# Attention and two mixtures of experts on one core: the first batch of attention by itself with host-laid operands, and a last dense expert without GpSimd splits

## The chip, the core and the metric

The kernel runs on one NeuronCore of a Trainium2 chip. The metric is the device time of one execution in microseconds (us). Before the change the median of three runs is 691.0 us.

The engines are named as in the profile: PE (TensorE, matrix products), PEld (its weight loads), DVE (VectorE), ACT (ScalarE), POOL (GpSimd) and SP (SyncE, which here only issues transfers). Each engine takes its instructions in the order of the program and waits, at the head of its queue, for what that instruction needs.

## The reference

Three stages follow each other. Sizes: 2 batches, 8 heads, 576 positions, head size 64; 1152 tokens of 512 features; 4 dense and 8 routed experts of 1024 hidden features.

```python
# attention, per batch and head (D = 64, scale = 1/8)
q_d, k_d, v_d = means over groups of 4 positions
out_up = np.repeat(softmax(scale * q_d @ k_d.T) @ v_d, 4, axis=positions)
mask = np.abs(pos[:, None] - pos[None, :]) < 4
out = out_up + softmax(np.where(mask, scale * q @ k.T, -1e9)) @ v
# dense experts, x of (1152, 512)
out = sum over e of p[:, e:e + 1] * (np.maximum(x @ w1[e], 0) @ w2[e])    # p: domain_probs, normalized
# routed experts
logits = (x / |x|) @ (emb / |emb|).T / tau
e = argmax(logits); out = softmax(logits)[e] * (np.maximum(x @ w1[e], 0) @ w2[e])
```

## The kernel before

**Precision.** All products are made in fp32. A weight or activation is split into a rounded half `hi` and the rest `lo`, and three products stand for one. `Weights.halves` (L378) makes one half-chunk (128x512) of a split: ACT writes `hi` (L390) and DVE or POOL writes `lo` (L394). Weights come in chunks of 512 KB into four `raw` buffers and are split into a ring of 13 slots; when both halves of a chunk are split, the next load is issued on SP (L374).

**Attention** (class `Attention`, L30). A unit is one batch and two heads; there are 8 units, 4 to a batch. The work of a unit is cut into 39 pieces, and the list `ROUND` is an order written out by hand: round i goes through the list and does each piece `name` for unit i - lag. `run` (L50) is a generator that makes one piece at a time. For a unit, k and q are loaded as rows (L72), turned on TensorE (twelve transposes of 96x128, L107), and copied out as `kT` and `qT` by ACT and DVE (L121, L127; q is scaled there). POOL adds groups of four positions of k, q and v (L142, L143, L157, L159). TensorE makes the banded scores of 9 blocks in two banks (five and four) and the pooled scores (L162, L187); DVE takes maxima, ACT the exponentials with their sums, DVE inverts the sums (L239, L240), POOL scales the weights (L251), TensorE turns them (L264, L281), ACT and DVE copy them out, TensorE multiplies by v (L306, L319), DVE adds (L332), and ACT and DVE split the result into `xh` and `xl` (L345, L350).

**Attention and the dense work.** At first attention runs alone: 257 of the 312 pieces, until all units of the first batch are done and most of the others well on. Then the dense experts begin. Expert 0 has chunks of 2, 2, 3 and 2 token tiles; the first two need the first batch only. They are 32 steps: `first_half` is one `l1` (12 matmuls), `second_half` is the `l2` of the f before. The other 55 pieces of attention are spread over the first 24 of these steps:

```python
while done < min(rest, -(-rest * (step + 1) // 24)):
    next(run)
    done += 1
if W.half < 2 * n_a:
    W.halves(1, "a", "v")
```

`l1` (L497) is evicted by ACT (L510) and DVE (L511), and `l2` (L513) adds over f = 0 to 7 into banks that L526 or L528 writes out.

**The last dense expert and the routing.** Experts 1 to 3 have three chunks of three tiles. In expert 3 the routing of a finished chunk runs beside the next one. `chunk_jobs` (L927) makes 16 lists of jobs, two for each f, and `step_jobs` does one list in each half of an f. A list can hold dot products of the tokens with the expert rows on DVE (`dots`, L743), the norms on POOL (L644 to L649), `choose` (L748), `ranks` on TensorE, `places` on DVE (L789: the one-hot tables `ohp` and `ohc`, L800 to L802), `enter` on TensorE (L809) and `early_tile`, which gathers the rows of the first two routed tiles with POOL (L854). The array `at` says in which list each job stands. In the same f's, ten chunks of weights of the routed experts are split, ACT for `hi` and POOL for `lo`. After the last dense step come the turns of the gathered rows (L1043), the last `l2`, and the routing of the last chunk, where logits are made on TensorE (L717, L732) and two more chunks are split (`W.halves(4, "vvaa", "p")`).

**The routed experts** follow, with layers at L1055 and L1023, tiles of 128 tokens and a branch for small counts.

Of the kernel before, what the change touches and what calls it, by code (L numbers as in the profile page):

```python
# [26 lines left out]
NRAW = 4  # L27


class Attention:  # L30
# [4 lines left out]
    ROUND = [  # L35
        ("value_a", 4), ("value_b", 4), ("value_d", 4), ("pool_v", 3), ("keep_q", 2), ("scores_a", 2), ("exp_b", 3),
        ("pool_k", 2), ("max_d", 3), ("sum_l", 3), ("scores_b", 2), ("lo", 5), ("max_a", 2), ("keep_d", 4),
        ("exp_d", 3), ("load_q", 1), ("pool_q", 2), ("exp_a", 2), ("scale_a", 3), ("scale_b", 3), ("sum_d", 3),
        ("scores_d", 2), ("turn_pa", 3), ("keep_pa", 3), ("load_vw", 2), ("scale_d", 3), ("add_a", 4), ("turn_pb", 3),
        ("add_b", 4), ("hi", 4), ("turn_pd", 3), ("turn_k", 1), ("turn_q", 1), ("load_k", 0), ("load_vg", 1),  # L40
        ("keep_pb", 3), ("keep_k", 1), ("keep_pd", 3), ("max_b", 2),
    ]

    def __init__(self, nc, cst, ld, wk, bank, q, k, v, xh, xl, pT):
        self.nc, self.cst, self.ld, self.wk, self.bank = nc, cst, ld, wk, bank
        self.q, self.k, self.v, self.xh, self.xl, self.pT = q, k, v, xh, xl, pT
        self.units = [(b, hp) for b in range(B) for hp in range(H // 2)]
        self.st = {}

    def run(self):  # L50

        rounds = len(self.units) + max(lag for _, lag in self.ROUND)
        for i in range(rounds):
            for name, lag in self.ROUND:
                u = i - lag
                if 0 <= u < len(self.units):
                    getattr(self, name)(u, self.st.setdefault(u, {}))
                    yield name, u
# [7 lines left out]
    def load_k(self, u, d):  # L66
        d["kn"] = self.load_rows(u, self.k, "kn")

    def load_q(self, u, d):
        d["qn"] = self.load_rows(u, self.q, "qn")  # L70

    def load_rows(self, u, src, tag):  # L72
        b, hp = self.units[u]
        t = self.ld.tile([96, 6, 2, D], F32, tag=tag, name=tag, bufs=2)
        for h in range(2):
            self.nc.sync.dma_start(out=t[:, :, h, :], in_=src[b, 2 * hp + h].rearrange("(j r) d -> j r d", r=6))
        return t

    def load_vg(self, u, d):
        nc, ld = self.nc, self.ld  # L80
        b, hp = self.units[u]
        vg = ld.tile([72, 2, 2, 4 * D], F32, tag="vg", name="vg", bufs=2)
        for h in range(2):
            nc.sync.dma_start(
                out=vg[:, :, h, :], in_=self.v[b, 2 * hp + h].rearrange("(a j r) d -> j a (r d)", a=2, r=4)
            )
        d["vg"] = vg

    def load_vw(self, u, d):
        nc, ld = self.nc, self.ld  # L90
        b, hp = self.units[u]
        vw = ld.tile([72, 9, 2, D], F32, tag="vw", name="vw", bufs=2)
        for h in range(2):
            off = ((b * H + 2 * hp + h) * S + 60) * D
            nc.sync.dma_start(
                out=vw[:, 1:8, h, :],
                in_=bass.AP(tensor=self.v.tensor, offset=off, ap=[[D, 72], [64 * D, 7], [1, D]]),
            )
        vs = self.v[b, 2 * hp:2 * hp + 2]
        nc.sync.dma_start(out=vw[0:68, 0], in_=vs[:, 0:68, :].rearrange("h p d -> p h d"))  # L100
        nc.sync.dma_start(out=vw[0:68, 8], in_=vs[:, 508:576, :].rearrange("h p d -> p h d"))
        d["vw"] = vw

    def turn(self, src, spots):
        ident = self.cst["ident"]
        for r, (t, o) in enumerate(spots):
            self.nc.tensor.transpose(t[:, o:o + 96], src[:, r].rearrange("p h d -> p (h d)"), ident[0:96, 0:96])  # L107

    def turn_k(self, u, d):
        d["tk"] = self.bank(), self.bank()  # L110
        self.turn(d["kn"], [(d["tk"][0], 96 * r) for r in range(5)] + [(d["tk"][1], 0)])

    def turn_q(self, u, d):
        d["tq"] = self.bank()
        self.turn(d["qn"], [(d["tk"][1], 96 + 96 * r) for r in range(4)] + [(d["tq"], 96 * r) for r in range(2)])

    def spread(self, T, t, o, r0, r1):
        src = t[:, o:o + 96 * (r1 - r0)].rearrange("p (r j) -> p r j", j=96)
        return T.rearrange("p (j r) -> p r j", r=6)[:, r0:r1, :], src

    def keep_k(self, u, d):  # L121
        kT = self.wk.tile([128, S], F32, tag="kT", name="kT", bufs=1)
        for t, o, r0, r1, e in ((d["tk"][0], 0, 0, 5, "a"), (d["tk"][1], 0, 5, 6, "a")):
            self.copy(e, *self.spread(kT, t, o, r0, r1))
        d["kT"] = kT

    def keep_q(self, u, d):  # L127
        qT = self.wk.tile([128, S], F32, tag="qT", name="qT", bufs=1)
        for t, o, r0, r1, e in ((d["tk"][1], 96, 0, 4, "a"), (d["tq"], 0, 4, 6, "v")):
            dst, src = self.spread(qT, t, o, r0, r1)  # L130
            if e == "a":
                self.nc.scalar.activation(out=dst, in_=src, func=AF.Copy, scale=0.125)
            else:
                self.nc.vector.tensor_scalar(out=dst, in0=src, scalar1=0.125, scalar2=None, op0=ALU.mult)
        d["qT"] = qT

    def fours(self, engine, T, out):

        e = self.nc.gpsimd if engine == "p" else self.nc.vector
        Tv = T.rearrange("p (g r) -> p g r", r=4)  # L140
        t = self.wk.tile([128, 144, 2], F32, tag="pt", name="pt")
        e.tensor_tensor(t, Tv[:, :, 0:2], Tv[:, :, 2:4], op=ALU.add)  # L142
        e.tensor_tensor(out, t[:, :, 0], t[:, :, 1], op=ALU.add)  # L143

    def pool_k(self, u, d):
        d["kd"] = self.cst["kd"][u % 2]
        self.fours("p", d["kT"], d["kd"][:, 0:144])

    def pool_q(self, u, d):
        d["qd"] = self.cst["qd"][u % 2]  # L150
        self.fours("p", d["qT"], d["qd"][:, 0:144])

    def pool_v(self, u, d):
        vg = d["vg"]
        e = self.nc.gpsimd if "p" == "p" else self.nc.vector
        t = self.wk.tile([72, 2, 2, 128], F32, tag="pv", name="pv")
        e.tensor_tensor(t, vg[:, :, :, 0:128], vg[:, :, :, 128:256], op=ALU.add)  # L157
        vd = self.wk.tile([72, 2, 2, D], F32, tag="vd", name="vd", bufs=2)
        e.tensor_tensor(vd, t[:, :, :, 0:64], t[:, :, :, 64:128], op=ALU.add)  # L159
        d["vd"] = vd  # L160
# [20 lines left out]
    def scores_a(self, u, d):  # L181
        self.scores(d, 0, 5)

    def scores_b(self, u, d):
        self.scores(d, 5, 9)
# [11 lines left out]

    def max_a(self, u, d):
        d["mx"] = self.wk.tile([128, 9], F32, tag="mx", name="mx", bufs=2)
        self.nc.vector.tensor_reduce(out=d["mx"][:, 0:5], in_=d["s0"], axis=AX.X, op=ALU.max, negate=True)  # L200

    def max_b(self, u, d):
        self.nc.vector.tensor_reduce(out=d["mx"][:, 5:9], in_=d["s5"], axis=AX.X, op=ALU.max, negate=True)

    def max_d(self, u, d):
        m = self.wk.tile([128, 3], F32, tag="mxd", name="mxd", bufs=2)
        self.nc.vector.tensor_reduce(out=m, in_=d["sd"], axis=AX.X, op=ALU.max, negate=True)
        self.nc.vector.tensor_scalar(out=m, in0=m, scalar1=1.0 / 16, scalar2=None, op0=ALU.mult)
        d["mxd"] = m

    def exp(self, P, src, bias, sm, scale=1.0):
# [4 lines left out]
    def exp_a(self, u, d):  # L216
        d["P"] = self.wk.tile([128, 9, 72], F32, tag="P", name="P", bufs=2)
        d["sm"] = self.wk.tile([128, 9], F32, tag="sm", name="sm", bufs=2)
        for i in range(5):
            sm = d["sm"][:, i:i + 1] if i < 5 else None  # L220
            self.exp(d["P"][:, i], d["s0"][:, i], d["mx"][:, i:i + 1], sm)

    def exp_b(self, u, d):
        for i in range(5, 9):
            sm = d["sm"][:, i:i + 1] if i < 5 else None
            self.exp(d["P"][:, i], d["s5"][:, i - 5], d["mx"][:, i:i + 1], sm)

    def exp_d(self, u, d):
        d["Pd"] = self.wk.tile([128, 3, 144], F32, tag="Pd", name="Pd", bufs=2)
        d["smd"] = self.wk.tile([128, 3], F32, tag="smd", name="smd", bufs=2)  # L230
        for i in range(3):
            sm = d["smd"][:, i:i + 1] if i < 3 else None
            self.exp(d["Pd"][:, i], d["sd"][:, i], d["mxd"][:, i:i + 1], sm, 1.0 / 16)

    def weights(self, P, sm, known, weight):

        if known < sm.shape[1]:
            self.nc.vector.tensor_reduce(out=sm[:, known:], in_=P[:, known:], axis=AX.X, op=ALU.add)
        self.nc.vector.tensor_scalar(out=sm, in0=sm, scalar1=1e-9, scalar2=weight, op0=ALU.add, op1=ALU.mult)  # L239
        self.nc.vector.reciprocal(sm, sm)  # L240
        return sm

    def sum_l(self, u, d):
        d["rc"] = self.weights(d["P"], d["sm"], 5, 1.0)

    def sum_d(self, u, d):
        d["rcd"] = self.weights(d["Pd"], d["smd"], 3, 4.0)

    def scale(self, engine, P, rc):
        e = self.nc.gpsimd if engine == "p" else self.nc.vector  # L250
# [1040 lines left out]
```

## Time and profile before

| | before |
|---|---|
| median of 3 runs | 691.0 us (689.84 to 691.18) |
| the profiled execution | 684.17 us, span 682.4 us, mean granted clock 0.997 |
| busy, share of the span | PE 95%, PEld 84%, DVE 51%, ACT 38%, POOL 21% |
| transfers | 73.58 MB in 53790 packets, of them 32286 under 512 B |

The span is the time from the first to the last instruction of the profiled execution. A row of the profile names the line, the engine, the operation, output and inputs with their shapes, the count, and then busy time, the mean of one in ns, and the idle time of the engine just before with what ended it. Busy times of matmuls overlap, so the distance between two starts is the better measure of what one costs. Times in rows count from the start of the span.

### The profile page before, as it was taken

To read this page: it belongs to the slowest core of one execution; us is meant where nothing else is said; L and a number is where in the kernel's file an instruction comes from. 1 tells how busy PE (TensorE), PEld (TensorE's weight loads), DVE (VectorE), ACT (ScalarE), POOL (GpSimd) and SP (SyncE) were. 2 spreads that over 40 slices of the span, in tenths; PEclk is the share of its full clock that TensorE was granted. 3 is DMA by queue.
4 is the path that set the end of the run, shared out by engine and by line. 5 is a ranking of instruction groups with operands and counts; after the bars stand their busy time and mean duration, and the time that the engine had idled before them with its cause. 6 is when DMAs were issued, how large, how long until landed. Compare 5 with 4: busy or idle time off the path is not lost. (4 is left out here: it accounts for less than half of the span.)

```text
span 682.4 us, 11487 instructions
## 1 busy us (share of the span) xinstructions
PE 648.9 (95%) x4287; PEld 574.6 (84%) x4287; DVE 346.3 (51%) x825; ACT 260.9 (38%) x653; POOL 145.1 (21%) x203
## 2 busy tenths in 40 slices
PE   5898999999999999999999999999799999999996
PEld 4677888998999999999999999999698877788775
DVE  2887763314442132442132327979663178499851
ACT  3777632112331111231111222243242368488752
POOL 4888411100000000000000001747441122112111
PEclk9999999999999999999999999999899999999999
DMA  8984430001231001130011116151562156499600
GB/s 222 214 190 117 110 97 2 2 0 37 88 123 62 1 12 50 30 130 27 1 31 63 62 63 200 60 177 62 180 250 79 32 187 214 163 324 361 240 20 30
DMA packets 53790, 73.58 MB, mean 108 GB/s; under 512 B 32286, under 2 KB 37678, under 8 KB 53696
## 3 DMA queue, kind: packets, MB, share of 16 engines
q1 hardware_dynamic: 51392, 66.09, 30.4%
q0 software_dynamic: 2304, 6.33, 3.2%
q8 instruction: 48, 0.79, 0.5%
q14 instruction: 46, 0.38, 0.2%
HBM read 66.10 MB, written 7.09 MB: 107 GB/s over the span
## 5 line engine op out<-in xcount | busy, mean ns | idle before, releaser
L520 PE MATMUL psb<-wh,hT 128*128 128x512 f32 x576 | 198.1, 396 | 0.0
L511 DVE SCALAR_TENSOR_TENSOR hT<-psb,hT 128x384 fp32r<-128x384 f32 (+1 forms) x104 | 54.7, 526 | 221.3 <-ACT hT L510 221.1
L510 ACT ACTIVATE hT<-psb 128x384 fp32r<-128x384 f32 (+1 forms) x104 | 48.5, 467 | 290.2 <-PE psb L506 290.1
L506 PE MATMUL psb<-xh,wh 128*128 128x384 f32 (+1 forms) x416 | 135.3, 325 | 0.0
L506 PE MATMUL psb<-xl,wh 128*128 128x384 f32 (+1 forms) x416 | 134.8, 324 | 0.0
L506 PE MATMUL psb<-xh,wl 128*128 128x384 f32 (+1 forms) x416 | 134.7, 324 | 0.0
L520 PEld LDWEIGHTS psb<-wh,hT 128*128 128x128 f32 x576 | 108.9, 189 | 20.9 <-issue 0.4
L520 PE MATMUL psb<-wl,hT 128*128 128x512 f32 x288 | 113.7, 395 | 0.0
L394 POOL TENSOR_TENSOR wl<-raw,wh 128x512 fp32r<-128x512 f32 x24 | 31.8, 1357 | 306.3 <-ACT wh L390 299.7
L506 PEld LDWEIGHTS psb<-xh,wh 128*128 128x128 f32 x416 | 78.1, 188 | 4.3
L506 PEld LDWEIGHTS psb<-xl,wh 128*128 128x128 f32 x416 | 78.2, 188 | 4.1
L506 PEld LDWEIGHTS psb<-xh,wl 128*128 128x128 f32 x416 | 78.2, 188 | 0.0
L394 DVE TENSOR_TENSOR wl<-raw,wh 128x512 fp32r<-128x512 f32 x108 | 72.6, 718 | 4.5 <-ACT wh L390 3.7
L390 ACT CAST wh<-raw 128x512 fp32r<-128x512 f32 x126 | 70.8, 624 | 0.1
L520 PEld LDWEIGHTS psb<-wl,hT 128*128 128x128 f32 x288 | 54.5, 189 | 7.9
L1055 PE MATMUL psb<-wh,gx 128*128 128x256 f32 x288 | 58.2, 288 | 0.3 <-ACT gx L1045 0.2
L1023 PE MATMUL psb<-wh,hT 128*128 128x512 f32 x160 | 53.9, 399 | 0.8 <-issue 0.5
L1055 PEld LDWEIGHTS psb<-wh,gx 128*128 128x128 f32 x288 | 46.2, 189 | 2.1 <-issue 1.3
L1055 PE MATMUL psb<-wl,gx 128*128 128x256 f32 x144 | 35.9, 283 | 0.0
L1023 PEld LDWEIGHTS psb<-wh,hT 128*128 128x128 f32 x160 | 30.1, 188 | 6.6 <-ACT hT L1006 0.5
L1023 PE MATMUL psb<-wl,hT 128*128 128x512 f32 x80 | 31.5, 394 | 0.0
L1055 PEld LDWEIGHTS psb<-wl,gx 128*128 128x128 f32 x144 | 27.2, 189 | 0.4
(250 smaller groups left out, 840.7 us busy)
## 6 DMA issues: line engine op xcount, KB each, us to landing
raw<-in_moe_w_dram SPq DMA_DIRECT2D x66, 512.0 KB
late_raw<-in_moe_w_dram SPq DMA_DIRECT2D x20, 512.0 KB
acc<-in_moe_w_dram SPq DMA_DIRECT2D x10, 512.0 KB
kn<-in_k_dram SPq DMA_DIRECT2D x16, 144.0 KB
qn<-in_q_dram SPq DMA_DIRECT2D x16, 144.0 KB
vg<-in_v_dram SPq DMA_DIRECT2D x16, 144.0 KB
rows<-acc SPq DMA_DIRECT2D x9, 256.0 KB
vw<-in_v_dram SPq DMA_DIRECT2D x16, 126.0 KB
```

The lines of the kernel that those rows point to most:

```text
L390: nc.scalar.copy(hi[:, c], t[:, c])
L394: lo_eng.tensor_tensor(lo[:, c], t[:, c], hi[:, c].bitcast(F32), op=ALU.subtract)
L506: nc.tensor.matmul(t, a[:, kk, fs], b_[:, kk, xs], start=(n == 0), stop=(n == 11))
L510: nc.scalar.activation(out=hi, in_=t, func=AF.Relu)
L511: nc.vector.scalar_tensor_tensor(out=lo, in0=t, scalar=0.0, in1=hi.bitcast(F32), op0=ALU.max, op1=ALU.subtract)
L520: nc.tensor.matmul(ys[t], a[:, ts], b_[:, f % 2, :], start=(f == 0 and j == 0), stop=(f == 7 and j == 2))
L1023: nc.tensor.matmul(y, gh[:, f, a], b_[:, f % 2, :], start=(n == 0), stop=(n == 23))
L1055: nc.tensor.matmul(dst, a[:, kk], w[:, kk, :], start=(n == 0), stop=(n == 11))
```

## The change

The host lays q and k out as [128, 576] for two heads, features on the partitions, and v as the two tables that the kernel reads; q, k and v of a unit come in two loads each, and the turns and copies of q and k go. The scale of q moves into the exponentials. `pool_q` becomes a reduction on DVE; sums and maxima are done by halves; `keep_d` and both parts of `dT` go to ACT. `ALONE` (34 pieces a unit) is the order for the four units of the first batch, which run alone to their end; `BESIDE` (36 pieces) is the order for the four units of the second batch, two pieces ahead of the dense work and the rest spread over 28 of the 32 steps. Four half-chunks are split in the alone part. In expert 3 the splits go from POOL to DVE, 11 chunks at places given by `AHEAD`, one chunk more after the counts; the routing of chunk 1 takes its third tile's logits on TensorE, and its later steps stand two or three lists earlier.

```diff
...
-    ROUND = [
...
+    ALONE = [
+        ("max_a", 1), ("sum_a", 2), ("scale_a", 2), ("value_d", 4), ("keep_d", 4), ("pool_v", 2),
+        ("turn_pa", 3), ("exp_d", 2), ("sum_b", 2), ("turn_pd", 3), ("value_b", 4), ("scores_a", 0), ("sum_d", 2),
+        ("add_a", 4), ("turn_pb", 3), ("add_b", 4), ("keep_pa", 3), ("keep_db", 3), ("pool_q", 0), ("pool_k", 0),
+        ("scores_b", 0), ("exp_a", 1), ("keep_8", 3), ("value_a", 3), ("scale_b", 2), ("keep_da", 3), ("scale_d", 2),
+        ("max_b", 1), ("max_d", 1), ("hi", 4), ("keep_pb", 3), ("scores_d", 0), ("lo", 4), ("exp_b", 1),
     ]
...
+    BESIDE = [
+        ("keep_pb", 6), ("scores_b", 4), ("max_b", 4), ("pool_k", 3), ("scores_a", 3), ("pool_v", 5), ("exp_a", 4),
...
+    def load_qk(self, u, d):
...
+        t = self.ld.tile([128, 2, S], F32, tag="qk", name="qk", bufs=3)
+        self.nc.sync.dma_start(out=t[:, 1, :], in_=self.k[b, hp])
+        self.nc.sync.dma_start(out=t[:, 0, :], in_=self.q[b, hp])
+        d["qT"], d["kT"] = t[:, 0, :], t[:, 1, :]
...
+        self.nc.vector.tensor_reduce(
+            out=d["qd"][:, 0:144], in_=d["qT"].rearrange("p (g r) -> p g r", r=4), axis=AX.X, op=ALU.add
+        )
...
+    def top(self, m, s, scale):
+
+        self.nc.vector.tensor_reduce(out=m, in_=s, axis=AX.X, op=ALU.max)
+        self.nc.vector.tensor_scalar(out=m, in0=m, scalar1=-scale, scalar2=None, op0=ALU.mult)
...
+    def sum_a(self, u, d):
+        self.inverse(d["sm"][:, 0:4], 1.0)
+
+    def sum_b(self, u, d):
+        self.nc.vector.tensor_reduce(out=d["sm"][:, 4:9], in_=d["P"][:, 4:9], axis=AX.X, op=ALU.add)
+        self.inverse(d["sm"][:, 4:9], 1.0)
...
+        self.copy("a", d["dT"][:, a].rearrange("p h (c q) -> p h c q", c=3), tv)
...
-        self.copy("v", d["od"], d["vo"][:, 0:144])
+        self.copy("a", d["od"], d["vo"][:, 0:144])
...
+        half = H // 2
+        W.ahead = 0
+        for name, u in (("load_qk", 0), ("load_qk", 1), ("load_qk", 2), ("load_v", 0), ("load_v", 1)):
+            att.load(name, u)
+        for name, u in att.run(att.ALONE, range(half)):
+            if name == "scores_d" and u == 0:
+                for name, u in (("load_qk", 3), ("load_v", 3), ("load_v", 2)):
+                    att.load(name, u)
                 W.load_to(NRAW)
...
+            elif name == "lo" and u < 3:
+                W.halves((1, 1, 2)[u], "a", "v")
+        W.ahead = NRAW
+        run = att.run(att.BESIDE, range(half, 2 * half))
+        rest, done = half * len(att.BESIDE), 2
+        next(run)
+        next(run)
...
-            while done < min(rest, -(-rest * (step + 1) // 24)):
+            while done < min(rest, -(-rest * (step + 1) // 28)):
...
-            s = acc[:, 2, :] if self.c == 2 and t == 2 else hs[:, 512 * (t % 2):512 * (t % 2) + 512]
+            s = xg if self.c == 1 else acc[:, 2, :] if t == 2 else hs[:, 512 * (t % 2):512 * (t % 2) + 512]
...
-        pairs = [(t, e) for t in range(3) for e in range(E2)]
+        pairs = [(t, e) for t in range(2 if c else 3) for e in range(E2)]
...
-        for i, m in enumerate(['3', '3', '3', '3', '3', '3', '2', '4'] if c == 0 else ['4', '1', '4', '3', '4', '3', '3', '2']):
+        for i, m in enumerate(['3', '3', '3', '3', '3', '3', '2', '4'] if c == 0 else ['4', '1', '4', '3', '4']):
...
-        at = [3, 7, 11, 12, 12, 14, 12, 15] if c == 0 else [3, 8, 11, 11, 11, 13, 14, 13]
+        at = [3, 7, 11, 12, 12, 14, 12, 15] if c == 0 else [3, 5, 8, 8, 8, 10, 12, 10]
         for i, j in zip(at, (r.norms, r.choose, r.ranks, r.places, r.count, r.enter, r.gates)):
...
+        if c == 1:
+            js[1].append(lambda: r.turn(2))
+            js[3].append(lambda: r.logits(2))
...
+    AHEAD = {(0, 5): 1, (0, 6): 1, (0, 7): 1, (1, 0): 1, (1, 1): 1, (2, 5): 2, (2, 6): 2, (2, 7): 2}
...
+                if e == E1 - 1 and (c, f) in AHEAD:
+                    W.split_to(W.split + AHEAD[c, f])
...
-                    elif f < 7:
-                        W.split_to(W.split + (1 if f == 1 else 2), "p")
-                elif e == E1 - 1 and c == 1 and f % 2 == 1:
-                    W.split_to(W.split + (1 if f < 7 else 2), "p")
...
-    W.halves(4, "vvaa", "p")
...
+    W.halves(2, "a", "v")
...
+    if name in ("q", "k"):
+        return a.reshape(B, H // 2, 2, S, D).transpose(0, 1, 2, 4, 3).reshape(B, H // 2, 128, S)
...
```

## Rows read from the trace of the kernel before

**Rows 1.** Busy time by stage: stretch, length, then busy us by engine, clock, DMA

```profile
70.31:122.89 52.58, 52.58 (x433) 47.24 (x430) 29.67 (x70) 20.54 (x63) 10.45 (x18) 1.00 0.24 68
122.89:415.20 292.31, 292.31 (x1508) 265.59 (x1507) 86.85 (x154) 60.51 (x123) 2.88 (x15) 1.00 0.15 49
415.20:478.60 63.40, 63.39 (x330) 57.16 (x328) 58.66 (x177) 22.59 (x52) 38.49 (x46) 1.00 0.38 123
478.60:490.40 11.80, 7.96 (x30) 5.85 (x30) 7.83 (x27) 2.53 (x8) 4.77 (x5) 0.86 0.49 153
```

**Rows 2.** TensorE timeline, borders of the first dense chunks: start, us, what

```profile
70.31 0.39 PE L506 MATMUL psb<-xh,wh 128*128 128x256 f32 x1
...
120.10 0.28 PE L506 MATMUL psb<-xh,wh 128*128 128x256 f32 x1
...
122.89 0.34 PE L506 MATMUL psb<-xh,wh 128*128 128x384 f32 x1
```

**Rows 3.** Busy time in one round of attention alone (columns of rows 1)

```profile
45.33:53.90 8.57, 7.58 (x128) 6.10 (x126) 6.83 (x19) 6.70 (x29) 6.84 (x9) 1.00 0.69 162
```

**Rows 4.** TensorE's timeline, the turns of k, first and third unit

```profile
4.89 1.19 PE L107 MATMUL psb<-ident,kn 96*128 96x96 f32 x6 [4.89 <-DMA kn<-in_k_dram]
...
24.27 0.66 PE L107 MATMUL psb<-ident,kn 96*128 96x96 f32 x6
```

**Rows 5.** Groups by form over two rounds: busy us, mean ns | idle before

```profile
L132 ACT ACTIVATE qT<-psb 128x384 f32<-128x384 f32 x2 | 1.7, 861 | 0.0
...
L142 POOL TENSOR_TENSOR pt<-qT 128x288 f32<-128x288 f32 x2 | 1.3, 666 | 0.2
...
L200 DVE TENSOR_REDUCE mx<-psb 128x5 f32<-128x360 f32 x2 | 1.1, 528 | 0.0
L134 DVE TENSOR_SCALAR qT<-psb 128x192 f32<-128x192 f32 x2 | 1.0, 506 | 0.5 <-PE psb L107 0.5
...
L64 DVE COPY dT<-psb 72x288 f32<-72x288 f32 x2 | 0.9, 454 | 0.1
...
L208 DVE TENSOR_SCALAR mxd<-mxd 128x3 f32<-128x3 f32 x2 | 0.9, 434 | 0.1
L143 POOL TENSOR_TENSOR qd<-pt 128x144 f32<-128x144 f32 x2 | 0.8, 425 | 0.2
...
L64 DVE COPY od<-psb 128x144 f32<-128x144 f32 x2 | 0.6, 298 | 0.0
```

**Rows 6.** TensorE timeline, end of expert 3; last, 2 us of busy time

```profile
476.30 0.34 PE L506 MATMUL psb<-xh,wh 128*128 128x384 f32 x1
...
481.42 1.83 PE L809 MATMUL psb<-ohc,ohp 128*128 128x144 f32 x6 [2.83 <-DVE ohc L802]
...
487.85 0.63 PE L1043 MATMUL psb<-ident,xg 128*128 128x128 f32 x4 [0.74 <-DMA xg<-rows_a,idx]
488.23 0.47 PE L520 MATMUL psb<-wh,hT 128*128 128x512 f32 x1
...
490.40 0.60 PE L1043 MATMUL psb<-ident,acc 128*128 128x128 f32 x4
...
484.00:486.00 2.00, 2.00 (x6) 1.54 (x6) 0.47 (x5) 1.36 (x6) 1.37 (x2) 0.50 0.09 35
```

**Rows 7.** DVE timeline, routing of chunk 1; last, a group of POOL

```profile
477.68 1.27 DVE L800 TENSOR_SCALAR ohp<-iota_p,sl 128x128 f32<-128x128 f32 x1
...
481.29 0.28 DVE L800 TENSOR_SCALAR ohp<-iota_p,sl 128x128 f32<-128x128 f32 x1
...
L394 POOL TENSOR_TENSOR wl<-raw,wh 128x512 fp32r<-128x512 f32 x24 | 31.8, 1357 | 306.3 <-ACT wh L390 299.7
```

**Rows 8.** DVE's groups over the whole span: busy us, mean ns

```profile
L511 DVE SCALAR_TENSOR_TENSOR hT<-psb,hT 128x384 fp32r<-128x384 f32 (+1 forms) x104 | 54.7, 526 | 221.3 <-ACT hT L510 221.1
L394 DVE TENSOR_TENSOR wl<-late_raw,wh 128x512 fp32r<-128x512 f32 x40 | 25.0, 686 | 0.4 <-ACT wh L390 0.3
...
L743 DVE SCALAR_TENSOR_TENSOR waste<-acc,xh 128x512 bf16<-128x512 f32 x12 | 8.4, 696 | 0.0
```

More of the change, by code (lines that the diff above doesn't have):

```diff
@@ L47, in __init__, with load, run @@
         self.units = [(b, hp) for b in range(B) for hp in range(H // 2)]
+        self.room = room
         self.st = {}
[L50 to L56, printed above, removed]
+    def load(self, name, u):
+        getattr(self, name)(u, self.st.setdefault(u, {}))
+    def run(self, order, units):
+        for i in range(len(units) + max(lag for _, lag in order)):
+            for name, lag in order:
+                if 0 <= i - lag < len(units):
+                    u = units[i - lag]
                     getattr(self, name)(u, self.st.setdefault(u, {}))
@@ L79, in load_vg @@
-    def load_vg(self, u, d):
-        nc, ld = self.nc, self.ld
-        b, hp = self.units[u]
[L82 to L135, printed above, removed]
@@ L551 @@
             nc.gpsimd.memset(t[:, 144:160], 0.0)
-        pT = acc[0:72, 4:9, :].rearrange("p t d -> p (t d)")[:, 0:2304].rearrange("p (n i c) -> p n i c", n=2, i=9)
-        att = Attention(nc, cst, ld, wk, bank, q, k, v, xh, xl, [pT[:, i] for i in range(2)])
+        acc_f = acc[0:72].rearrange("p t d -> p (t d)")
+        pT = acc_f[:, 2304:4608].rearrange("p (n i c) -> p n i c", n=2, i=9)
+        room = {3: dict(vw=acc_f[:, 0:1152], vg=acc_f[:, 1152:2176])}
+        att = Attention(nc, cst, ld, wk, bank, q, k, v, xh, xl, [pT[:, i] for i in range(2)], room)
         nc.gpsimd.dma_start(out=pr, in_=probs.rearrange("(t p) e -> p t e", p=128))
-        pieces = len(att.units) * len(att.ROUND)
-        run = att.run()
-        first = 0
-        for n, (name, u) in enumerate(run, 1):
-            if n == 14:
-                W.load_to(NRAW)
-            if n >= 20 and (n - 20) % 8 == 0 and W.half < 4:
-                W.halves(1, "v", "v")
-            if name == "lo" and u == H // 2 - 1:
-                first = n + 36
-            if n == first:
-                break
+        half = H // 2
[6 more added lines that the diff above has]
+                    att.load(name, u)
+                W.load_to(NRAW)
+            elif name == "lo" and u < 3:
[5 more added lines that the diff above has]
+        next(run)
         nc.vector.tensor_reduce(out=psm, in_=pr, axis=AX.X, op=ALU.add)
@@ L570 @@
         nc.vector.tensor_tensor(pr, pr, psm.unsqueeze(2).to_broadcast([128, NT, E1]), op=ALU.mult)
-        W.halves(max(0, 4 - W.half), "v", "v")
-        rest, done = pieces - first, 0
         for step in range(32):
```

153 lines of the change are left out of this document (78 added, 75 removed).

## The prediction

> **What bounds the kernel now.** I read the stage table first (busy time per engine over stretches that I cut at the borders of the stages), then TensorE's timeline at those borders, then the groups by form in one attention round. The stage table [rows 1] shows TensorE busy all the time wherever dense experts run: 52.58 of 52.58 us while the last attention pieces run beside expert 0, and 63.39 of 63.40 us in the last 63 us of expert 3. Work taken off another engine there is worth nothing by itself. TensorE is short in three places: before the dense work (attention alone, up to 70.31 us [rows 2]); in the 11.80 us from 478.60, where it works 7.96 us [rows 1]; and after 490.40 us, which the change hardly touches.
>
> Attention alone moves in rounds of 8.57 us, and in one round no engine is full: DVE 6.83, POOL 6.84, ACT 6.70 [rows 3]. What they wait for is each other; the fill of the busiest is 6.84/8.57 = 0.80. Beside dense work the matter is different: TensorE is the bound, and attention costs only what it puts in TensorE's queue. So the change is a trade: it moves attention from a stage that lasts as long as its rounds to one that lasts as long as its matmuls.
>
> **Beside the dense work.** One l1 and one l2 of a two-tile chunk take 122.89 - 120.10 = 2.79 us [rows 2], 1.395 a step; the 31 steps from 70.31 to 122.89 are 43.2 us. The stretch took 52.58, so attention added 9.4 us. The orders written in the code put 55 of 312 pieces there, 39 to a unit: 1.41 units, 6.65 us a unit, waits included. That stands close to the 7.58 us of TensorE in a round less its twelve turns, 2 x 0.66 us (the six of k in the third unit [rows 4], and six of q like them): 6.3 us. After, four whole units lie there: 4 x 6.65 = 26.6 us, so the stretch is 43.2 + 26.6 = **69.8 us**. Ends: 68.4 with 6.3 a unit; the upper end is the rival on DVE.
>
> **Attention alone.** Removed per unit [rows 5]: twelve turns on TensorE; ACT's scaled copy of q (0.86) and the two copies of k beside it; on DVE the copies of q (0.51), dT (0.45) and od (0.30), of which ACT takes back dT and od; on POOL the two adds that pool q (0.67 and 0.43). Added on DVE: pool_q as one reduction over 576 columns, which no row shows: the reduction of 360 columns takes 0.53 and bounds it from below, 0.53 x 576/360 = 0.85 from above; I take 0.75, nearer the longer one. Then two small scalings after the maxima and, as the sums are split, one more scaling and one more reciprocal; a small scaling takes 0.43 with POOL at work [rows 5], so the four are 0.8 to 1.7, and I take 1.1, since a reciprocal reads as few elements. DVE per unit: 6.83 - 1.26 + 0.75 + 1.1 = 7.4 us. POOL falls to 5.75, ACT to about 5. **DVE is the busiest.** Four units and four early splits of 0.69 each [rows 8] are 32.4 us of DVE.
>
> The start: the first k, 288 KB in two transfers, is there at 4.89 us [rows 4]; q and k in one layout are 2 x 295 KB, so scores begin at 5 to 8; I take 5.5. TensorE is slow then: the same six turns take 1.19 us at 4.89 and 0.66 at 24.27 [rows 4]. Two units of scores at that pace, and DVE's first maxima, put the third round at about 13 us with 3.5 us of DVE's work done. The other 28.9 us at a fill of 0.85 (above the 0.80 of now, as ACT and POOL have fewer pieces to be waited for) take 34: **the dense work starts at 47 us**. Ends: 10 + 28.9/0.95 = 40; and, if the pace stayed at 8.57 for five rounds and the last took 3, 13 + 42.9 + 3 = 59.
>
> Queues passed: on SP the load of v of unit 2 waits for POOL to have pooled unit 0, and the four weight loads wait behind it; their first reader is the split after lo of unit 0, which comes in the fifth round. Beside the dense work the load of q and k of unit 7 waits for the scores of unit 4, with later v behind it, one round early. With `W.ahead` at 0, chunk 4 is loaded only from the second split beside the dense work, six steps before it is read. I cost these at nothing; if the cover goes, each is one 512 KB load, 4 us at the 123 GB/s of a stretch with such loads [rows 1].
>
> Together 47 + 69.8 = 116.8 instead of 122.89: **6.1 us gained**. That is a small remainder of two large terms: 23 us earlier, 17 us longer.
>
> **The last dense expert.** TensorE starts the last l1 at 476.30, ends it at 478.59, and waits 2.83 us for `ohc` of the routing [rows 6]. DVE was late because its ordinary 0.28 us operations took 1.27 while POOL ran its splits, 1.36 us each, 24 of them [rows 7]. After that wait the granted clock is 0.50, which is 1.2 GHz [rows 6], the following matmuls run slowly, and TensorE waits 0.74 more for the gathered rows. From 476.30 to 490.40 are 14.10 us. Without waits: l1 2.1, l2 2.17 (488.23 to 490.40), the turns 0.38 (487.85 to 488.23), l2 2.17: 6.8 us; the six matmuls of `enter`, now three steps earlier, 0.9, half of their 1.83; new are four turns, 0.38, and four short matmuls of logits, which I put at 0.8, twice that, since each also loads weights. Sum 8.9; gain 5.2.
>
> DVE's side: 8 dots go, 8 x 0.70, 22 splits come, 22 x 0.69 = 15 us [rows 8], six of them in a chunk of the long stretch where DVE has 86.85 us of work in 292.31 [rows 1], four in the next, twelve in the last three f (8.3 us in 3 x 4.27 = 12.8, with the end of the routing). The queue is full there, and the evictions of l1 and the lower half of the gathered rows stand behind splits: I leave 1.2 us of new TensorE waits, ends 0 and 3. The two gathers on POOL go out three steps earlier and past eight fewer splits; the five earlier weight loads pass the row stores on SP, which have many microseconds. The four splits taken from the routing of the last chunk, and the two put after the counts, lie beside TensorE's next layer and cost nothing; uncovered, 1.4 us. **Net 4.0 us**, ends 1 and 6.
>
> **Sum.** 10.1 us. The profiled execution took 684.17 us (span 682.4 and 1.8 around it) and would take 674.1. The median of the runs is 691.0, 6.8 above it; I carry that over: **681 us**.
>
> **Rivals.**
> *The clock in the thinner stage.* Alone, TensorE would hold some 25 us of work in 47, where it is now busy 7.58 of 8.57 us. A 2.83 us wait was followed by 0.50 [rows 6], and the first turns ran at half pace. If it stays slow, a unit is 6.3 x 1.19/0.66 = 11.4 us of TensorE, which then bounds the stage: 5.5 + 4 x 11.4 + 3 = 54, a time of 688. For: turns and scores come in short bursts. Against: a slow engine is busier, and the granted clock over the round of now is 1.00 [rows 3]. The Trainium skill (page "TensorE: Matmul & The Clock Gate", part 1) says that half clock is the default and that activity alone lifts it, which speaks against this part of the change; the wait at 478.59 agrees with it. Chance 0.15.
>
> *The routing's wait only moves.* The gathers or the lower half of the rows come late behind DVE's twelve splits, and the 4.0 us are lost: 685. Chance 0.11.
>
> *Slower: DVE holds up the dense work.* Beside it each f carries 10.3 of a unit's 36 pieces, 2.1 us of DVE, its own eviction (0.53 [rows 8]) and, in the first six f, two splits: 4.0 us in TensorE's 2.79 + 26.6/14 = 4.7. An eviction stands in DVE's queue behind pieces that wait for ACT. At the fill of 0.80 an f takes 4.0/0.80 = 5.0, 6 x 0.3 = 2 us in all, which the 6.65 may hold already; at 0.55 it takes 7.3, 6 x 2.6 = 15 us: 681 + 15 - 2 = 694. It turns slower below a fill of about 0.61, where an f takes 6.6. For: alone the engines do wait so. Against: TensorE did not idle in this stretch with DVE at 29.67 of 52.58 [rows 1]. Chance 0.10.
>
> *More:* rounds at a fill of 0.95 give 40 us and 674. Chance 0.08.
>
> **Numbers.** The forecast, with starts of 44 to 51 us, has 0.56 and its own range is 677 to 685. The range of 673 to 689 takes in the better case, the clock and the moved wait, and leaves out the slower one. What 0.2% (1.4 us) separates is about all that a measurement of this kernel can tell from no change. Faster: 0.56 + 0.11 + 0.08 and most of the clock's 0.15, 0.87; same 0.04; slower 0.09.
>
> **To be seen afterwards.** The first dense matmul near 47 us (40 to 51; at 59 the alone part is wrong); expert 0's third chunk near 117, TensorE still without idle time between; DVE the busiest engine of the alone stage, the granted clock there at 1.00; no wait for `ohc` before `enter`, gathers landed before the turns, the clock at 1.00 throughout, `ohp` at 0.28. From turn_x to the end the profile should be as long as now, about 192 us from the second turn; if that part moves by over 2 us, the prediction left something out.

## The result and the profile after

The median went from 691.09 us (686.38 to 692.92, six runs) to **681.06 us** (676.28 to 685.76, six runs); the ratio is 0.986, 95% interval 0.983 to 0.989. The profiled execution took 676.28 us with a span of 674.6, against 684.17 and 682.4. So the profiled one gained 7.9 us and the median 10.0. One run of all that follow, the 685.22 us of e3_fill, counts as slow, being over 1.5% above that kernel's fastest; without it the two medians that hold it, 675.39 and 676.8 us, are 674.8 and 676.0.

| us from the span's start | before | after | predicted |
|---|---|---|---|
| first dense matmul | 70.31 | 39.40 | 47 |
| from there to expert 0's third chunk | 52.58 | 77.46 | 69.8 |
| third chunk of expert 0 | 122.89 | 116.86 | 116.8 |
| from there to the second turn | 367.51 | 363.82 | 363.5 |
| from the second turn to the end | 192.0 | 193.9 | 192 |
| mean granted clock of the profiled run | 0.997 | 0.992 | 1.00 in the stages changed |
| packets of all transfers | 53790 | 25500 | |

Busy time by stage in the changed kernel (columns of rows 1): the stage alone, cut at 13 us, the stage beside expert 0, the last 12 us before the second turn, and the rest.

```profile
0.00:13.00 13.00, 8.93 (x136) 7.03 (x138) 7.91 (x23) 5.95 (x28) 6.99 (x19) 1.00 0.82 228
13.00:39.40 26.40, 21.37 (x306) 16.64 (x303) 23.27 (x59) 18.24 (x75) 19.80 (x26) 0.94 0.74 222
...
39.40:116.86 77.46, 75.17 (x721) 63.11 (x719) 48.11 (x119) 35.73 (x131) 23.07 (x32) 0.96 0.31 96
...
468.58:480.68 12.10, 11.97 (x63) 10.36 (x62) 9.40 (x25) 7.73 (x19) 2.54 (x2) 1.00 0.56 182
480.68:674.60 193.92, 178.04 (x1174) 153.94 (x1172) 117.86 (x289) 107.53 (x225) 38.98 (x42) 1.00 0.50 177
```

Alone, VectorE (third busy column) is the busiest: 7.91 + 23.27 = 31.2 of 39.4 us. Beside expert 0 TensorE is busy 75.17 of 77.46, no longer all the time as in [rows 1], and the clock is 0.96. In the end of the last dense expert the idle time is gone: 11.97 of 12.10 at full clock, where [rows 1] have 7.96 of 11.80 at 0.86.

TensorE's timeline in the changed kernel: the first l1, then the scores beside it, and the end of expert 3.

```profile
39.40 0.39 PE L473 MATMUL psb<-xh,wh 128*128 128x256 f32 x1
...
42.18 0.38 PE L473 MATMUL psb<-xh,wh 128*128 128x256 f32 x1 [1.45 <-ACT xh L72]
42.97 0.58 PE L473 MATMUL psb<-xl,wh 128*128 128x256 f32 x1 [0.41 <-DVE xl L318]
...
44.05 1.21 PE L133 MATMUL psb<-qk 64*64 64x68 f32 x16
...
468.58 0.90 PE L785 MATMUL psb<-ohc,ohp 128*128 128x144 f32 x6
...
477.76 0.60 PE L1022 MATMUL psb<-ident,xg 128*128 128x128 f32 x4
```

The first l1 starts before the last unit's result is split, and waits 1.45 and 0.41 us for the two halves. At the other end neither `enter` (468.58) nor the turns of the gathered rows (477.76) wait any more; [rows 6] have 2.83 and 0.74 there.

The clock in the changed kernel, in short stretches (columns of rows 1).

```profile
27.00:30.00 3.00, 1.98 (x15) 1.63 (x16) 2.97 (x6) 3.00 (x15) 0.62 (x1) 0.81 0.96 358
30.00:33.00 3.00, 3.00 (x34) 2.22 (x34) 2.86 (x9) 2.18 (x11) 2.24 (x3) 0.62 0.79 303
...
42.00:44.00 2.00, 1.42 (x4) 0.79 (x4) 1.44 (x5) 0.32 (x2) 0.00 (x0) 0.62 0.00 0
44.00:46.00 2.00, 2.00 (x24) 1.50 (x25) 1.70 (x4) 1.21 (x3) 0.00 (x0) 0.50 0.03 8
46.00:48.00 2.00, 2.00 (x23) 1.87 (x21) 1.49 (x6) 0.00 (x0) 0.00 (x0) 0.50 0.00 0
48.00:50.00 2.00, 2.00 (x14) 1.73 (x15) 0.43 (x1) 0.26 (x1) 0.00 (x0) 0.67 0.92 296
```

Behind the waits of the first l1 the granted clock stands at 0.50, which is 1.2 GHz, until about 49 us. The sixteen score matmuls at 44.05 take 1.21 us there, against 0.71 us for the same sixteen at a clock of 1.00 in e3_fill (below).

VectorE's groups over the whole span of the changed kernel (busy us, mean ns).

```profile
L361 DVE TENSOR_TENSOR wl<-raw,wh 128x512 fp32r<-128x512 f32 x132 | 86.1, 700 | 3.9 <-ACT wh L357 3.3
...
L108 DVE TENSOR_REDUCE qd<-qk 128x144 f32<-128x576 f32 x8 | 5.9, 741 | 2.3 <-DMA qk<-in_q_dram 2.3
L195 DVE TENSOR_SCALAR smd<-smd 128x3 f32<-128x3 f32 x8 | 5.1, 632 | 1.0 <-ACT Pd L175 1.0
...
L776 DVE TENSOR_SCALAR ohp<-iota_p,sl 128x128 f32<-128x128 f32 x9 | 2.6, 284 | 0.0
```

The new reduction costs 0.74 us (0.75 was taken), and `ohp` is at 0.28 in all nine, as it was once POOL was quiet in [rows 7].

### The profile page after: what moved, and what is told of

Its sections match the earlier page's. It is cut to its first block, busy times and chain, and to the rows that moved or that the text cites. A ratio compares the mean times of both kernels' runs of the same rounds, so it can differ in the third digit from the quotient of the medians.

```text
span 674.6 us, 11209 instructions
## 1 busy us (share of the span) xinstructions
PE 646.6 (96%) x4203; PEld 569.3 (84%) x4203; DVE 345.4 (51%) x844; ACT 254.3 (38%) x644; POOL 105.5 (16%) x163
## 2 busy tenths in 40 slices
DMA packets 25500, 73.58 MB, mean 109 GB/s; under 512 B 3102, under 2 KB 6190, under 8 KB 25408
## 5 line engine op out<-in xcount | busy, mean ns | idle before, releaser
L473 PE MATMUL psb<-xh,wh 128*128 128x384 f32 (+1 forms) x416 | 137.0, 329 | 1.5 <-ACT xh L72 1.5
L361 DVE TENSOR_TENSOR wl<-raw,wh 128x512 fp32r<-128x512 f32 x132 | 86.1, 700 | 3.9 <-ACT wh L357 3.3
L357 ACT CAST wh<-raw 128x512 fp32r<-128x512 f32 x132 | 74.4, 624 | 0.1
L615 POOL TENSOR_TENSOR rsq<-ss,nr 128x3 f32<-128x3 f32 x9 | 3.3, 370 | 341.9 <-DVE nr L613 323.7
```

Source lines behind the costliest of these rows:

```text
L357: nc.scalar.copy(hi[:, c], t[:, c])
L361: lo_eng.tensor_tensor(lo[:, c], t[:, c], hi[:, c].bitcast(F32), op=ALU.subtract)
L473: nc.tensor.matmul(t, a[:, kk, fs], b_[:, kk, xs], start=(n == 0), stop=(n == 11))
L615: eng.tensor_tensor(t, ss, y, op=ALU.mult)
```

## The experiments

The theory at this point: the stage alone is bound by VectorE, the stage beside by TensorE with a loss to its clock, and the end of the last dense expert by splits on GpSimd. Rivals: the two offsets at 40 us have another cause, the clock loss is no price of the change, and the gain at the end is that of the moved routing steps. Each series had the kernel before on its own chip, with medians from 690.3 to 691.2 us. "The middle part" is the distance from expert 0's third chunk to the second turn.

**The two parts by themselves.** e1_attention is the changed attention with the last expert and its routing as before; e2_late the opposite.

```diff
...
-                    W.split_to(W.split + AHEAD[c, f])
+                    elif f < 7:
+                        W.split_to(W.split + (1 if f == 1 else 2), "p")
...
-        at = [3, 7, 11, 12, 12, 14, 12, 15] if c == 0 else [3, 5, 8, 8, 8, 10, 12, 10]
+        at = [3, 7, 11, 12, 12, 14, 12, 15] if c == 0 else [3, 8, 11, 11, 11, 13, 14, 13]
...
```

> The attention part of the change alone, the end of expert 3 as before. Theory A (the two parts add up, each with what its own stretch of the trace shows): third chunk of expert 0 at about 117 us, against 122.9 before; time 5 to 7 us under the kernel before. Rival B (what the medians show beyond the profiled execution belongs to the attention part, whose clock differs from run to run): more than 7 us under, with run times that spread by 5 us or more and follow the mean granted clock.

Measured: 682.01 us (681.03 to 688.93), ratio 0.9881 (0.9842 to 0.992), so 8.9 us under before, more than theory A's 5 to 7; third chunk at 118.05 us, middle part 367.68, unchanged. That is rival B's case: the runs spread by 7.9 us and follow the mean granted clock, from 681.03 us at 0.991 to 688.93 at 0.973. Before's own runs lose to the clock too (see below).

> The last part of the change alone: attention as before, no GpSimd splits beside expert 3, routing steps moved. Theory A: 3 to 4 us under the kernel before between expert 0 and the second turn (367.5 before, 364 expected), and 0 to 2 us given back behind it; time 2 to 4 us under. Rival B: nothing, because the time behind the second turn grows by as much: within 1 us.

Measured: 689.46 us (686.66 to 693.0), ratio 0.9977 (0.9954 to 1.0), so 1.4 us under before, between the two theories. The middle part took 363.72 us, as theory A said and as in the changed kernel, but the stretch after it 196.3.

The gains of 8.9 and 1.4 add up to the 10.0 of both: to within the spread of runs the parts do not lean on each other. In the middle the late part saves its 3.8 us by itself, but its median gained less. What follows the second turn varies: it took 192.0 us in the profile of before, 194.3 in another execution of the same code there (e8 below), 196.8 in e1, whose code there is also that of before, and 193.7 to 197.4 in the others. What moves are single waits of TensorE, of 0.7 to 2.1 us, at changing places; the longest one for gathered rows is 1.2 us in before, 1.65 in e2 and under 0.8 in e3, and others are for small tables on VectorE or have no releaser in the profile. The 192.0 of before was the low end of that.

**The clock.** e3_fill puts idle matmuls, which nothing reads, where TensorE waits just before and at the first dense matmul.

```diff
+        JUNK = {("scale_a", 3): 5, ("lo", 1): 3, ("lo", 3): 6}
         for name, u in att.run(att.ALONE, range(half)):
+            if (name, u) in JUNK:
+                spare = bank()
+                for _ in range(JUNK[name, u]):
+                    nc.tensor.matmul(spare[:, 0:128], ident, ident, start=True, stop=True)
```

> The changed kernel with 14 idle matmuls (identity times identity, results unread) in three places where TensorE waits at the end of the attention alone: before the third, the fourth and after the last unit's products. Theory A (TensorE's waits there drop its clock to half, and the slow time is paid in the first steps of the dense work): granted clock stays at 1.00 from 30 to 55 us, the third chunk of expert 0 starts 2 to 4 us earlier than 116.9, and the runs spread less. Rival B (the clock is low but TensorE has slack or waits for DVE there anyway): third chunk at 116 to 118, no gain or up to 1 us of loss for the added matmuls.

Measured: **675.39 us** (672.37 to 685.22), ratio 0.9776 (0.9737 to 0.9815). Stretches of its trace (columns of rows 1):

```profile
42.00:44.00 2.00, 1.59 (x20) 1.10 (x20) 1.68 (x6) 0.71 (x2) 0.00 (x0) 1.00 0.00 0
44.00:46.00 2.00, 2.00 (x32) 1.72 (x29) 1.88 (x5) 0.70 (x2) 0.00 (x0) 1.00 0.00 0
46.00:48.00 2.00, 2.00 (x34) 1.73 (x34) 1.67 (x5) 1.20 (x8) 0.00 (x0) 1.00 0.61 183
...
40.54:114.23 73.69, 72.29 (x721) 60.86 (x720) 45.83 (x116) 35.30 (x129) 23.13 (x32) 1.00 0.36 101
```

In this execution the clock does not fall from 30 to 55 us; with dense work starting 1.1 us later, the third chunk comes 2.6 us earlier, and the stretch beside is 3.8 us shorter. To see whether this was the chip, the changed kernel and this one ran once more side by side.

> The changed kernel, unaltered, beside its copy with 14 idle matmuls on the same chip, since they were measured on different chips so far. Theory A (the fall of the clock around the first dense matmul costs the changed kernel some 3 to 6 us in most of its runs): median 680 to 683 us, mean clocks of 0.978 to 0.992. Theory B (the 5.7 us were the chip's): within 2 us of its copy with idle matmuls.

> The changed kernel with the 14 idle matmuls of e3_fill. Theory A: median 674 to 677 us, 3 us or more under the changed kernel's on the same chip, most mean clocks at 0.995 or more. Theory B: within 2 us of it.

Measured: 680.35 us (676.26 to 684.9), ratio 0.985 (0.981 to 0.989), and 677.79 us (674.04 to 680.09), ratio 0.9792 (0.976 to 0.9824). The difference is 2.6 us, under the 3 us that theory A asked for, and the two intervals overlap. In the second kernel's profile the clock fell elsewhere, to 0.60 at 14 to 18 us, to 0.66 at 36 to 40 and again at 488 to 492, and its dense work began at 43.51 us instead of 40.54:

```profile
36.00:40.00 4.00, 4.00 (x41) 3.02 (x37) 2.44 (x4) 1.71 (x5) 3.16 (x5) 0.66 0.00 0
```

What repeats from execution to execution is the stage beside the dense work: 73.5 to 74.0 us in the five profiles with idle matmuls at the border and the same work behind it (e3, e6, e9, e10, e12), 76.4 to 77.8 us in the five without (the changed kernel, e1, e4, e5, e11). Over all 12 runs of each the medians are 680.8 and 676.8: holding the clock there is worth about **4 us** to the changed kernel, with what the idle matmuls themselves cost taken off; 2.6 to 5.7 by the single series. The idle matmuls make a fall rarer, not impossible.

Two more kernels bound this. e8_before_fill is the same idea in the kernel before.

```diff
+        JUNK = {("scores_d", 1): 4, ("turn_pa", 0): 3, ("turn_pd", 0): 5, ("turn_k", 3): 6}
...
```

> A control: the kernel before with 18 idle 128x128 matmuls put where TensorE stood still in the first 27 us of its attention (ahead of turn_pa and turn_pd of unit 0, scores_d of unit 1 and turn_k of unit 3). Theory A (the clock's fall is a price of the thinner stage that the change makes): within 1.5 us of the kernel before's own median, ratio 0.998 to 1.003. Theory B (both kernels lose as much to it): 3 us or more under the kernel before, ratio 0.996 or less, with the mean granted clock of its runs nearer to 0.997 than to 0.987.

Measured: 689.43 us (688.32 to 694.93), ratio 0.9991 (0.9965 to 1.0017). The ratio is theory A's and the difference, 1.65 us, is a little over its 1.5. That does not show that the 4 us are a price of the thinner stage. In e8's own profile the clock is 1.00 through the attention, and still the first dense matmul comes at 72.14 us, 1.8 later than in [rows 2], so these idle matmuls have a price of their own there, and what a held clock gave back does not come out of the difference; and its 12 runs still have mean clocks of 0.983 to 0.995. Before loses to the clock as well, at other places: the profile of e2, whose attention is that of before, shows 0.50 from 30 to 34 us and its first dense matmul 3.7 us later than [rows 2], and before's profiled execution at 0.997 took 6.9 us less than its median. Which kernel loses more to the clock stays open.

> The changed kernel with 33 idle matmuls in nine places of the stage alone (e3_fill: 14 in three): also ahead of lo of units 0 and 2, of scale_a of unit 2 and of value_d of units 1 to 3. Theory A (what is left of the spread between runs in e3_fill, 672 to 685 us, are further falls of the clock in this stage): no run above 679 us, median 673 to 675, all mean clocks at 0.995 or more. Theory B (VectorE bounds the stage, the clock is already held, and the spread comes from elsewhere): a median within 1.5 us of 675.4 and still single runs over 679 us with a clock under 0.99.

```diff
...
+            ("scale_a", 2): 4, ("scale_a", 3): 5, ("lo", 0): 3, ("lo", 1): 3, ("lo", 2): 3, ("lo", 3): 6,
+            ("value_d", 1): 3, ("value_d", 2): 3, ("value_d", 3): 3,
...
```

Measured: 680.3 us (677.2 to 682.45), ratio 0.9849 (0.9813 to 0.9886). Neither theory. The spread narrowed from 7.7 us (e3_fill without its 685.22) to 5.3 us and five of six clocks lie at 0.994 or more, but the first dense matmul came at 44.47 us, with VectorE's work unchanged:

```profile
0.00:44.47 44.47, 37.10 (x503) 30.39 (x503) 32.85 (x85) 25.63 (x105) 26.88 (x44) 1.00 0.68 199
```

TensorE works 37.1 us there, 32.70 in e3_fill. Idle matmuls ahead of `value_d` and `lo` stand in the chain of a unit; in this kernel they held the clock and cost more than it.

**What bounds the stage alone, and the stage beside.** From here on the base is e3_fill, whose first profile has a clock of 1.00 through both stages. Its stage alone, and 28 us from within it, in which VectorE (third busy column) is busy 25.18:

```profile
0.00:40.54 40.54, 32.70 (x465) 26.01 (x465) 33.05 (x83) 24.76 (x104) 26.80 (x44) 1.00 0.75 218
...
8.00:36.00 28.00, 24.32 (x345) 18.83 (x344) 25.18 (x66) 20.73 (x97) 20.17 (x26) 1.00 0.86 248
```

e6 and e7 repeat the reduction of pool_q, with the same result, in the first and in the last four units.

```diff
+        for _ in range(3 if u < 4 else 1):
+            self.nc.vector.tensor_reduce(
...
```

> The changed kernel with the idle matmuls (e3_fill), and pool_q's reduction done three times for the first four units: 2 x 0.75 us of VectorE added to each unit of the stage alone, 6.0 us in all, nothing else. Theory A (the prediction's: VectorE bounds the stage alone): the first dense matmul comes 4.5 to 6 us later than e3_fill's 40.54 us, at 45 to 46.5 us. Theory B (the chain of one unit through TensorE, ScalarE and GpSimd bounds it, and VectorE has room): under 2.5 us later, at 43 us or before.

> The same three reductions for the last four units, whose attention runs beside dense expert 0: 6.0 us of VectorE added there. From the first dense matmul to the third chunk of expert 0 e3_fill took 73.69 us. Theory A (TensorE's own work bounds that stage): 73.5 to 75 us. Theory B (VectorE holds up the evictions, the prediction's slower rival in a milder form): 77 to 80 us.

Measured, e6 (rows of its trace: the stage alone, the same 28 us, and the stretch behind them) and then e7:

```profile
0.00:45.94 45.94, 36.27 (x464) 28.55 (x465) 38.94 (x91) 24.96 (x104) 26.76 (x44) 0.93 0.66 192
...
8.00:36.00 28.00, 24.31 (x325) 18.74 (x321) 26.90 (x66) 19.43 (x92) 16.52 (x21) 0.94 0.86 251
...
36.00:40.00 4.00, 2.25 (x14) 1.71 (x15) 3.53 (x8) 1.76 (x4) 3.84 (x6) 0.72 0.01 2
```

```profile
40.43:115.90 75.47, 72.59 (x721) 60.86 (x720) 51.14 (x124) 35.16 (x129) 23.10 (x32) 1.00 0.33 98
```

Of 6.0 us of VectorE added alone, 5.4 appear in the first dense matmul (45.94 - 40.54). But e6's clock was not steady: it fell to 0.72 from 36 to 40 us, where e3_fill has 1.00. Just before that, VectorE's first addition of the second unit (`add_a`) starts at 36.28 us instead of 32.50, 3.8 later, and the other 1.6 come behind the fall. Against e12, e3_fill's program with its clock falling at the same place, e6 starts its dense work 2.4 us later (45.94 - 43.51). So 2.4 to 3.8 of the 6.0 us are VectorE's, which is between the two theories. Together with the rows above this says that VectorE bounds the stage up to about 36 us: there the added work first fills its gaps (26.90 busy us of 28 instead of 25.18) and the rest shows as time. Behind that the chain of the last units sets the pace, and TensorE's clock with it. Beside the dense work 1.8 us appear (75.47 - 73.69), both at a clock of 1.00 and nearer to theory A: VectorE bounds that stage only here and there, and TensorE idles 2.9 us instead of 1.4. The medians, of two runs each, are 681.85 and 677.87 us.

e10 goes the other way and gives pool_q of the first four units back to GpSimd:

```diff
+        if u < 4:
+            t = self.wk.tile([128, 144, 2], F32, tag="pt", name="pt")
+            self.nc.gpsimd.tensor_tensor(t, Tv[:, :, 0:2], Tv[:, :, 2:4], op=ALU.add)
+            self.nc.gpsimd.tensor_tensor(d["qd"][:, 0:144], t[:, :, 0], t[:, :, 1], op=ALU.add)
+            return
...
```

> e3_fill with one part of the change undone for the first four units: pool_q goes back to two adds on GpSimd, 0.75 us of VectorE less and 1.1 us of GpSimd more a unit. Theory A (VectorE bounds the stage alone, in both directions): the first dense matmul at 37.5 to 39 us instead of 40.54, median 1.5 to 3 us under e3_fill's 675.4. Theory B (GpSimd's added work lengthens VectorE's small instructions and the chain through it, and gives it back): the first dense matmul at 40 us or later, median within 1 us of e3_fill's or above.

Measured: 680.68 us (678.13 to 684.6), ratio 0.9862 (0.9824 to 0.9899).

```profile
0.00:42.44 42.44, 34.63 (x464) 27.26 (x465) 30.28 (x79) 24.85 (x104) 31.08 (x52) 0.96 0.66 208
```

VectorE has 2.8 us less to do than in e3_fill (33.05 in its first 40.54 us), and the stage is 1.9 us longer; GpSimd is now the busiest with 31.08. The 1.9 us are no fall of the clock: they are there at 16.84 us, where the pooled scores of the third unit have waited 2.55 us for GpSimd's sums of k and start 2.0 us later than in e3_fill (14.86), and the clock falls only behind that, to 0.68 from 16 to 20 us. Theory B: relief of the bounding engine was worth nothing where the work went to the next one. The move of pool_q to VectorE is right.

**The end of the last dense expert.** e4 keeps all of the change but gives the moved splits back to GpSimd.

```diff
-                    W.split_to(W.split + AHEAD[c, f])
+                    W.split_to(W.split + AHEAD[c, f], "p")
```

> The changed kernel with the lower halves of the 11 chunks split beside expert 3 put back on GpSimd; all routing steps stay where the change put them. Theory A (GpSimd's splits slow DVE's short operations from 0.28 to over 1 us, but with the steps moved forward there is room for it): no wait before enter, time within 1 us of the changed kernel, since TensorE is the bound. Rival B (taking the splits off GpSimd is what removed the wait): the wait for ohc before enter comes back with 2 us or more, and the time is 2 to 5 us above the changed kernel.

Measured: 685.67 us (683.4 to 688.98), ratio 0.994 (0.9912 to 0.9968); middle part 370.30 us. The time is rival B's; the place of the wait is not, since `enter` ran at 469.90 without waiting, as theory A said. Its timelines of VectorE, GpSimd, ScalarE and TensorE:

```profile
474.23 5.42 DVE L795 SCALAR_TENSOR_TENSOR nb<-m,nr 128x3 f32<-128x3 f32 x1
...
473.62 0.97 POOL L830 DMA_INDIRECT acc<-rows_a,idx  x1 [0.30 <-issue]
474.61 5.01 POOL L361 TENSOR_TENSOR wl<-raw,wh 128x512 fp32r<-128x512 f32 x4
...
479.69 0.39 ACT L797 ACTIVATE ez<-z,nb,nr 128x8 f32<-128x8 f32 x1 [6.17 <-DVE nb L795]
...
483.71 0.80 PE L487 MATMUL psb<-wh,hT 128*128 128x512 f32 x1 [4.03 <-ACT hT L477]
```

One VectorE instruction of three columns, 0.16 us elsewhere in the changed kernel, takes 5.42 us and ends when four GpSimd splits have ended. The exponential that needs it follows, the eviction of l1 stands behind that on ScalarE, and TensorE waits 4.03 us. The Trainium skill ("SBUF — State Buffer", section "SBUF: two separate sides") says that VectorE, in an instruction with two tensor inputs, and GpSimd take one port pair by an exclusive lock, held for the whole instruction; these rows agree that one of the two is kept waiting. By their times VectorE's instruction started first, 0.38 us before the first split and while GpSimd was at a gather, and it still ended only with the fourth: no run here shows why it got no turn between them.

e5 does the reverse: the splits stay on VectorE, the routing steps go back to where they stood, and the logits of the third tile from TensorE to dot products on VectorE.

```diff
...
-        at = [3, 7, 11, 12, 12, 14, 12, 15] if c == 0 else [3, 5, 8, 8, 8, 10, 12, 10]
+        at = [3, 7, 11, 12, 12, 14, 12, 15] if c == 0 else [3, 8, 11, 11, 11, 13, 14, 13]
...
```

> The changed kernel with the routing steps of the third chunk put back where they stood in the kernel before, while the splits of the last dense expert stay off GpSimd (on VectorE). Theory A: the splits on GpSimd were what lengthened the last dense expert (with them back the third chunk of expert 0 to the second turn took 370.3 us against 363.8), and the moved steps are worth little: from the third chunk to the second turn 363.5 to 365.5 us and a median within 2 us of the changed kernel's 681.06. Theory B: half the gain is the moved steps': 366.5 us or more from the third chunk to the second turn, a wait of TensorE for the table ohc ahead of enter, median 684 us or more.

Measured: 685.84 us (683.89 to 687.48), ratio 0.9932 (0.9905 to 0.9959); middle part 369.73 us. Theory A falls, and the times are theory B's. VectorE's, GpSimd's and then TensorE's timeline:

```profile
474.05 2.50 DVE L361 TENSOR_TENSOR wl<-raw,wh 128x512 fp32r<-128x512 f32 x4
...
476.93 0.30 DVE L836 COPY tab_a<-psb 128x144 f32<-128x144 f32 x1
...
478.28 1.10 POOL L830 DMA_INDIRECT xg<-rows_a,idx  x1 [13.74 <-DVE nb L795]
...
482.64 1.09 PE L1019 MATMUL psb<-ident,xg 128*128 128x128 f32 x4 [5.66 <-DMA xg<-rows_a,idx]
```

`enter` ran at 473.90 without a wait for `ohc` (theory B expected one). But VectorE made four splits and an eviction before it copied out the table that `enter` had written (476.93), so the first gather was issued at 478.28, and its rows came 5.66 us after TensorE was ready. In the changed kernel the first gather is issued here:

```profile
470.88 1.57 POOL L830 DMA_INDIRECT xg<-rows_a,idx  x1 [9.32 <-DVE wl L361]
```

The four middle parts make one table: 367.5 us with neither, 370.3 with the steps moved and GpSimd splitting, 369.7 with VectorE splitting and the steps unmoved, 363.8 with both; each is of one profile, and where the code is the same the part repeats within 1 us (367.5 to 368.0 in three executions, 363.1 to 363.9 in nine). **Each alone loses 2 to 3 us; together they gain 3.7.**

## Why the prediction was right, and where it was only lucky

**The total** fits, 681.06 against 681.0, and the profile shows that two large misses cancel in it: 7.6 us too long alone, 7.7 too short beside. That the sum is right to 0.1 us there is luck. The start of the dense work lies outside the forecast's 44 to 51 us; it is that of the case "More" (40 us), whose time of 674 did not come, since the stage beside gave the gain back.

**Alone: 39.40 us, 47 predicted; VectorE as the bound was right up to about 36 us (its rows, and e6).** Its work was nearly right too: 31.2 us, 1.2 of them preparation before 3.1 us that the sum did not have, against 32.4. What failed is the start: the prediction let the third round begin at 13 us "with 3.5 us of DVE's work done"; on VectorE it began at 9.62, and 7.91 us were done by 13. So 23.27 us were left instead of 28.9, which at the fill of 0.85 is 6.6 us. The fill itself was 23.27/26.4 = 0.88, another 1.0. The slow first matmuls, which the prediction took from [rows 4], held TensorE up, but VectorE could work behind them.

**Beside: 77.46 us, 69.8 predicted.** The term that failed is 6.65 us a unit, "waits included": by the prediction's own reckoning, with 43.2 us of dense steps, a unit took 34.3/4 = 8.6. Attention's own matmuls did cost what was said, 26.6 us for four units: the distances between starts on TensorE, summed over attention's lines, are 26.7, though in part at half clock (25.3 in e3). The missing 7.7 us lie in the dense work and in idle time. Idle are 2.3 us, mostly the first l1 at the border, for which the prediction had nothing. The first two l1 take 4.30 us (1.86 of it idle) and 2.65 us by their distances instead of 1.395, in part at half clock: 2.3 us. And a dense step between attention's matmuls takes 1.5 to 1.6 us, some 3.0 us over the stretch: 1.395 had come from steps at its end, where nothing lies between them [rows 2]. At full clock (e3) the stretch is 73.69, so about half of the 7.7 is the clock and what hangs on it: of these 3.8 us, 2.8 are matmuls that ran faster and 1.0 is idle time.

**The clock** was a rival with a chance of 0.15, and it came true in another form. The stage alone did not become a TensorE stage of 54 us; the clock was mostly 1.00 there. It fell to 0.62 from 30 to 33 us and to 0.50 from 44 to 48 behind the waits of the first l1, and cost about 4 us (e3, e12). The sentence "the granted clock there at 1.00" was wrong, and with it the silence of the sum on the clock. The Trainium skill ("TensorE: Matmul & The Clock Gate", part 1) says that activity alone lifts the clock; e3 agrees, since matmuls without any use kept it at 1.00 in its first profile.

**The last dense expert: net 4.0 predicted, 3.7 measured** (3.8 in e2). The waits for `ohc` and for the gathered rows are gone, the clock is 1.00 to the second turn, and of the 1.2 us left for new waits 0.6 came at 422 us, for an eviction in VectorE's queue, and 0.1 before the last l2. The rival "the routing's wait only moves" is what e5 is, in its mechanism (gathers late behind VectorE's splits) and in its time (685.84 us, 685 said); in e4 the wait moves to an eviction. Either happens if only one of the two edits is made. The prediction priced the two as one and did not say that each needs the other; e4 and e5 show it.

**After the second turn** 193.9 us for 192: inside the 2 us allowed, and inside the spread of that stretch.

**The sum against its own execution** gave 674.1 where 676.28 was measured; the median's gain was 10.0 because before's median lay 6.9 us above its profiled execution and after's only 4.8. **VectorE holding up the dense work** (0.10) did not come: even 6 us more of it there cost 1.8 (e7).

## What to carry to other kernels

When work leaves a stage bound by its chain for a stage bound by TensorE, price the border between them: who has to finish before the first instruction of the second stage, and what TensorE's clock does while it waits. Two edits around one wait can each lose and together win, so test them singly and together before either is dropped. A few idle matmuls exactly where TensorE waits at such a border were worth about 4 us here, and more of them, inside the chain of a unit, lost that again.

## What the runs showed that was not expected

A VectorE instruction on 128x3 elements took 5.42 us beside four GpSimd splits in a row (0.16 without), and in attention the 128x3 scaling of `smd` took 0.63 us on average, its like on 128x4 0.16. A run's time follows its mean granted clock: the changed kernel's six runs go from 676.28 us at 0.992 to 685.76 at 0.978. The best version measured is the changed kernel with 14 idle matmuls, 676.8 us over 12 runs, and its spread (672.37 to 680.09 us, without the 685.22) shows that the clock is not fully held even so.
